# Decay products of a recurrent attention kernel from logarithms and a triangular product in place of scans

## The chip, the cores and the metric

One core of one Trainium2 chip. The metric is device time in microseconds of one launch; the median of three runs is quoted. The profile shows the core's engines: TensorE (PE, its weight loads apart as PEld), VectorE (DVE), ScalarE (ACT), GpSimd (POOL) and the DMA issuing queue of SyncE (SP). Each engine works through its own instructions strictly in their order and waits on semaphores for the others.

## The reference

First comes a recurrent attention over 768 steps for 4 batches of 8 heads with 40 by 40 states, then a mixture of experts, top 2 of 8, on its output:

```python
for t in range(S):                       # per batch and head
    y[:, :, t] = einsum('bhd,bhde->bhe', rt, state)
    Sa = einsum('bhde,bhe->bhd', state, at)
    state = state * wt[:, :, None, :] - einsum('bhd,bhe->bhde', Sa, bt) + einsum('bhd,bhe->bhde', vt, kt)
# x = y as rows [3072, 320]
noisy = x @ w_gate + log1p(exp(x @ w_noise)) * noise     # the router
top2, softmax over the two
out[rows of e] += weight * (relu(x @ w1[e]) @ w2[e])      # F = 1024
```

The decays w lie between 0.85 and 0.95. Inside a chunk of 64 steps the kernel needs the running products of w over time and their reciprocals.

## The kernel before

The 768 steps are cut into 12 chunks of 64; a **unit** is one chunk of half of the batches (16 batch-heads), so that there are 24 units, u = 0 to 23. Most work of a unit runs as products of 64 by 64 tiles of fp32, four tiles of the array at once. One pass of the loop in `run` is **stage n**; it works on unit n and prepares unit n+8 (`LP=8`). The order in which the calls are written in `run` is the order of every engine's instructions (the schedule is manual); loads are tied to ScalarE instructions (`after`, `s.ea`).

The path of a unit: `TA`, `TB` finish the inverse of a triangular matrix, `U` uses it, `UT` transposes the result, `P` multiplies with r, VectorE masks that (`pm`, L743), and `Y` of the same unit, at the start of the next stage, gives the output rows and the new state S. `RL` turns the output into rows and adds the router's logits. `AK`, `KBT`, `W1`, `W2`, `ST` feed these. TensorE and ScalarE alternate along this path: each product is evicted from PSUM by ScalarE before the next.

The decays: `scans` (L578 to L582) on VectorE makes the reverse running product B, the reciprocal of its ends, and the forward running product wq. `aprod` and `kprod` multiply a, k and b by these, and `LS` makes the matrix that is to be inverted; `LSe` evicts it by three ScalarE instructions out of PSUM. For four units at a time (a group) VectorE solves 32 by 32 triangles by 30 elimination steps of two operations each (`solve`, L619 and L620), spread over the four stages by the table `PLAN`, between a transposition into X (`xtr`) and two out of it (`tout`). The first group is solved in 16 by 16 halves (`solve16`) and completed by small products (`S16`) for each of its units.

Around the loop: `ramp` prepares units 0 to 4 and solves the first group; stage 0 then carries `S16` for units 1 to 3 and prepares units 5 to 8. The router (`gate_`, `route`) runs for 8, 4, 4, 4 and 4 units as a generator that is advanced by `m.rstep()` at three places of a stage. `warm` issues fp16 products on a zero tile, whose results nobody reads, on TensorE. Ten writes of zeros to the output (`zero`, 320 KB each) are issued in `ramp`, six later. After unit 23 the experts follow (from about 420 us), which the change doesn't touch.

## Time and profile before

| | |
|---|---|
| median of three runs | 832.08 us (830.48 to 838.36) |
| the profiled execution | 834.11 us, span 832.4 us |
| busy share of the span: PE, PEld, DVE, ACT, POOL | 87%, 63%, 67%, 44%, 37% |
| mean granted TensorE clock | 0.973 of 2.4 GHz |
| chain that ended last | PE 60%, DVE 22%, ACT 7%, issue 5%, DMA 2%, POOL 2% |
| the mask `pm` starts: units 1, 3, 9, 15, 23 | 86.35, 114.28, 200.24, 299.64, 417.19 us |

The start of the mask of unit n marks the end of stage n's TensorE path and is used as milestone throughout. A window of the profile gives busy time of each engine between two such marks; a timeline gives single instructions with their start, length and, in brackets, the idle time before them and what ended it. PE's records are two per fp32 product, and they overlap: the distance from start to start tells what a product costs.

### The profile page before, as it was taken

What the parts mean: (1) busy time and instruction counts of PE and PEld (TensorE: products, weight loads), DVE (VectorE), ACT (ScalarE), POOL (GpSimd) and SP (SyncE); (2) the same over time, 40 slices, a digit from 0 to 9 for tenths busy, and PEclk for the clock granted to TensorE, in tenths of its full rate; (3) what the DMA queues carried; (4) which work ended last, traced back from release to release, by engine and by line L of the source; (5) the groups of instructions that cost most, each with busy time, mean ns of one, the idle gap of its engine ahead of it and who ended that gap; (6) DMA issues with size and microseconds to landing.
All of it is one profiled execution on the core that took longest, in us unless ns stands there. A gap on an engine that the chain in (4) does not pass through costs nothing.

```text
span 832.4 us, 30024 instructions
## 1 busy us (share of the span) xinstructions
...
## 2 busy tenths in 40 slices
...
GB/s 214 242 182 59 153 135 151 155 143 119 108 114 117 114 94 90 66 127 122 68 96 65 163 70 154 144 141 93 142 29 149 75 124 120 36 18 24 29 17 40
DMA packets 67703, 89.54 MB, mean 108 GB/s; under 512 B 15640, under 2 KB 49388, under 8 KB 67564
## 3 DMA queue, kind: packets, MB, share of 16 engines
...
q0 software_dynamic: 12160, 17.15, 12.3%
q8 instruction: 105, 1.72, 0.9%
q14 instruction: 34, 0.28, 0.1%
HBM read 65.82 MB, written 21.69 MB: 105 GB/s over the span
## 4 chain that ended last, share of the span: by engine, by line
PE 60%; DVE 22%; ACT 7%; issue 5%; DMA 2%; POOL 2%; another core or an unknown queue 1%; SPq 0%; DVEq 0%; ACTq 0%; POOLq 0%
PE po L366 20%; PE ph L351 19%; DVE Tt L619 4%; DVE X__71 L620 3%; PE pp L740 3%; DVE pm L743 2%; PE kt L687 2%; PE pt L331 2%; PE py L760 2%; ACT la L523 2%; PE tb L673 2%; ACT tt L523 1%; DVE B L578 1%; PE ta L663 1%; DVE dr L623 1%
## 5 line engine op out<-in xcount | busy, mean ns | idle before, releaser
L374 POOL DMA_INDIRECT out_dram<-y,le x45 | 74.8, 1662 | 193.6 <-ACT y L368 189.4
L351 PE MATMUL ph<-rw__68,rk 128*128 128x384 f16 (+1 forms) x512 | 97.0, 339 | 3.6 <-DVE hl L353 1.7
L351 PE MATMUL ph<-dr,la 128*128 128x448 f16 (+1 forms) x384 | 86.7, 342 | 1.7 <-DVE rk L353 1.7
L366 PEld LDWEIGHTS <-rk 128*128 128x128 f16 x576 | 56.6, 100 | 38.5 <-issue 8.6
L179 POOL DMA_INDIRECT ls<-ent,po x48 | 48.6, 1013 | 77.8 <-ACT pm L523 43.2
L351 PEld LDWEIGHTS <-rk 128*128 128x128 f16 x512 | 49.4, 98 | 40.3 <-issue 4.1
L353 DVE SCALAR_TENSOR_TENSOR hl<-ph,hh 128x448 f16<-128x448 f32 x64 | 39.4, 623 | 48.1 <-ACT hh L352 46.1
L593 POOL TENSOR_TENSOR rk<-rk,B 104x512 f32<-104x512 f32 x32 | 37.9, 1184 | 85.2 <-DVE X__71 L620 36.0
L368 ACT ACTIVATE y<-po,le 128x320 f32<-128x320 f32 (+1 forms) x53 | 26.6, 504 | 94.1 <-PE po L366 75.2
L352 ACT ACTIVATE hh<-ph 128x448 f16<-128x448 f32 x64 | 34.2, 542 | 67.5 <-PE ph L351 64.0
L239 DVE TENSOR_REDUCE yc<-y 128x1 f32<-128x320 f32 (+1 forms) x53 | 23.9, 457 | 57.6 <-ACT y L368 52.0
L619 DVE TENSOR_TENSOR Tt<-X__71 128x30 f32<-128x30 f32 (+9 forms) x150 | 57.8, 385 | 4.1
L352 ACT ACTIVATE rk<-ph 128x384 f16<-128x384 f32 x64 | 30.8, 489 | 63.5 <-PE ph L351 48.0
L366 PEld LDWEIGHTS <-hh 128*128 128x128 f16 (+1 forms) x640 | 46.6, 103 | 18.7 <-issue 2.2
L353 DVE SCALAR_TENSOR_TENSOR rk<-ph,rk 128x384 f16<-128x384 f32 x64 | 34.3, 553 | 33.9 <-ACT rk L352 24.6
L351 PEld LDWEIGHTS <-la 128*128 128x128 f16 x384 | 37.6, 99 | 28.4 <-issue 3.0
L620 DVE TENSOR_TENSOR X__71<-X__71,Tt 128x30 f32<-128x30 f32 (+9 forms) x150 | 50.0, 333 | 5.5
L366 PE MATMUL po<-ra,rk 128*128 128x320 f16 x288 | 46.0, 306 | 3.0 <-ACT rk L352 2.5
L760 PE MATMUL py<-pm,kt 128*64 128x104 f32 (+1 forms) x768 | 42.0, 259 | 1.8 <-issue 0.9
L743 DVE TENSOR_TENSOR pm<-pp,mk 128x512 f32<-128x512 f32 x48 | 30.9, 685 | 16.0 <-PE pp L740 12.9
L600 PE MATMUL ls<-rk,ra 64*64 64x64 f32 x768 | 20.7, 251 | 23.9 <-DVE rk L593 8.7
L760 PEld LDWEIGHTS py<-pm,kt 128*64 128x64 f32 x768 | 36.2, 140 | 6.6 <-issue 3.1
...
## 6 DMA issues: line engine op xcount, KB each, us to landing
...
```

The costliest lines, as they stand in the source:

```text
L179: st=nc.gpsimd.indirect_dma_start(out=s.ls,out_offset=OFFS(ap=po[:,j,k:k+1],axis=0),in_=s.ent[:,j,k],in_offset=None)
L351: for i,(a,b) in enumerate(mm): s.hmm=nc.tensor.matmul(ph[:,:n],a,b,start=i==0,stop=i==7)
L352: s.hrelu=nc.scalar.activation(hh[:,f],ph[:,:n],AF.Relu)
L353: s.hhl=nc.vector.scalar_tensor_tensor(hl[:,f],ph[:,:n],0.0,hh[:,f],op0=ALU.max,op1=ALU.subtract)
L366: for j in range(c): nc.tensor.matmul(po[p*j:p*j+p,:d],h[:,f,r],w[:,f,d*j:d*j+d],start=k==0,stop=k==23)
L368: s.hy=nc.scalar.activation(y[:,:d],po[:,:d],AF.Copy,scale=w_[:,ii:ii+1])
L374: st=s.nc.gpsimd.indirect_dma_start(out=o[0],out_offset=OFFS(ap=o[1],axis=0),in_=o[2],in_offset=None,compute_op=ALU.add)
L593: s.after((eng or s.nc.gpsimd).tensor_tensor(z,z,b1,op=ALU.mult),e)
L619: eng.tensor_tensor(t,X[:,j:j+1,j+1:].to_broadcast([128,j,m]),X[:,0:j,j:j+1].to_broadcast([128,j,m]),op=ALU.mult)
L620: s.hs=eng.tensor_tensor(X[:,0:j,j+1:],X[:,0:j,j+1:],t,op=ALU.add)
L743: nc.vector.tensor_tensor(m[:,y,:,0:64],pp[:,y].rearrange("p (j t)->p j t",t=64),s.mk.to_broadcast([128,8,64]),op=ALU.mult)
L760: nc.tensor.matmul(pp[64*y:64*y+64,b,104*hh:104*hh+n],kt[:,j,y],m[:,y,j,0:n],start=first and hh==0,stop=True,skip_group_check=True)
```

## The change

It replaces the scans. The logarithm of w is taken on ScalarE (`ln`), a product with a 128 by 128 triangle of ones on TensorE sums it along time for all 8 heads of a unit (`sm`, four fp32 products of 128 by 128), and two exponentials on ScalarE give wq and B (`ex`). VectorE keeps the largest logarithm of each unit (`lc`) for the check at the end. w is loaded in another layout (160 KB a unit in place of 260).

Other edits: the second half of `LSe` is copied from the result in SBUF and moved later (`LSd`); the state is no longer added by an identity product but by VectorE, and scaled by GpSimd; `RL` uses four products of 128 rows in place of sixteen 64 by 64 tiles; the mask is one instruction; the router's arithmetic before the top 2 goes to GpSimd, save for the last four units; `PLAN` spreads the elimination steps otherwise, with a place C behind `Y`; the fill products in `UT` go where `sm` comes. `ramp` is rewritten, and stage 0 is a function of its own (`first`), written out by engine needs: `S16` of units 2 and 3 moves into stages 1 and 2, the first group's X is masked before its transposition, and six of the ten writes of zeros and the zeros of xd move into the loop.

```diff
+    def zx(s):
+        nc=s.nc; z=s.z; n=24-NA; return nc.sync.dma_start(s.xd[0][128*NA:3072].rearrange("(p a) (h d)->p (a h) d",p=128,h=2),z.rearrange("p (o d)->p o d",o=1).to_broadcast([128,2*n,DM//2]))
...
+        nc=s.nc; E=nc.vector if n0+T>=NT else nc.gpsimd
-        zc=r("zc"); nc.vector.tensor_scalar(zc,lg[:,:,8:16],41.0,None,op0=ALU.min)
+        zc=r("zc"); E.tensor_scalar(zc,lg[:,:,8:16],41.0,None,op0=ALU.min)
...
-PLAN={0:dict(A=range(1,8)),1:dict(B=range(8,11),A=range(11,15)),2:dict(B=range(15,19),A=range(19,25)),3:dict(B=range(25,31))}
+PLAN={0:dict(A=range(1,5)),1:dict(C=range(5,7),B=range(7,12),A=range(12,14)),2:dict(C=range(14,15),B=range(15,20),A=range(20,22)),3:dict(C=range(22,24),B=range(24,31))}
+PLAN1={1:dict(B=range(1,8),A=range(8,12)),2:dict(C=range(12,14),B=range(14,20),A=range(20,22)),3:dict(C=range(22,24),B=range(24,31))}
...
+        s.L=[t([128,4,2,64],F32,name="L"),s.uc]; s.TR=t([128,136],F32,name="TR")
+        G.memset(s.TR,0.0)
+        for b in range(2):
+            z=s.TR[64*b:64*b+64,64*b:64*b+64]; G.memset(z,1.0)
+            G.affine_select(out=z,in_=z,pattern=[[-1,64]],base=0,channel_multiplier=1,compare_op=ALU.is_ge,fill=0.0)
...
+    def ln(s,u):
+        s.act(s.L[u%2 if u<7 else 0][...,0:40],s.fl(s.wq[u%NW])[:,0:320].rearrange("p (h y e)->p h y e",h=4,y=2),AF.Ln)
+    def lc(s,u):
+        s.nc.vector.tensor_reduce(s.lm[:,u:u+1],s.L[u%2 if u<7 else 0][...,0:40].rearrange("p h y e->p (h y) e"),axis=AX.XY,op=ALU.max,apply_absolute_value=True)
+    def sm(s,u):
+        pp=s.Sp=s.p1t("sm"); L=s.L[u%2 if u<7 else 0]
+        for hh in range(4): s.nc.tensor.matmul(pp[:,128*hh:128*hh+128],L[:,hh].rearrange("p y e->p (y e)"),s.TR[:,0:128],start=True,stop=True)
+    def ex(s,u):
+        z=s.Sp.rearrange("p (j t)->p j t",t=64); B=s.B[u%2][:,0:520].rearrange("p (j c)->p j c",c=65)
+        s.act(s.wq[u%NW][:,:,0:64],z,AF.Exp,scale=-1.0)
+        s.act(B[:,:,0:64],z,AF.Exp)
+        s.nc.gpsimd.tensor_copy(s.gam[0:RF,u],B[0:RF,:,0])
     def scans(s,u):
...
+        s.ln(u); s.sm(u); s.ex(u)
...
     def LSe(s,u,pp):
         g,us=divmod(u,4); l=s.lab[g%2][:,8*us:8*us+8].rearrange("p (y h) t->p y h t",y=2); z=pp[:,:,0:256].rearrange("p y (h t)->p y h t",t=64)
         s.act(l,z,AF.Copy,scale=-1.0)
+    def LSd(s,u):
+        g,us=divmod(u,4); l=s.lab[g%2][:,8*us:8*us+8]
         for b in range(2):
-            r=slice(64*b,64*b+32); s.act(l[r,:,:,32:64],z[r,:,:,0:32],AF.Copy,scale=-1.0)
+            r=slice(64*b,64*b+32); s.act(l[r,:,32:64],l[r,:,0:32],AF.Copy)
...
     def UT(s,u):
-        nc=s.nc; pp=s.p1t("ut"); s.warm(pp,FU)
+        nc=s.nc
+        if u and u+LP<NU: s.sm(u+LP)
+        pp=s.p1t("ut")
+        if not u or u+LP>=NU: s.warm(pp,FU)
...
-        for y in range(2):
-            nc.vector.tensor_tensor(m[:,y,:,0:64],pp[:,y].rearrange("p (j t)->p j t",t=64),s.mk.to_broadcast([128,8,64]),op=ALU.mult)
+        nc.vector.tensor_tensor(m.rearrange("p y j x->p (y j) x")[...,0:64],pp.rearrange("p y (j t)->p (y j) t",t=64),s.mk.to_broadcast([128,16,64]),op=ALU.mult)
...
-            if not last:
-                for b in range(2):
-                    nc.tensor.matmul(pp[:,b,0:416].rearrange("p (h x)->p h x",x=104)[...,64:104],s.m.idm,S.rearrange("p (h b) d->p b h d",b=2)[:,b,:,0:40],start=False,stop=False,skip_group_check=True)
...
-            nc.vector.tensor_tensor(S.rearrange("p (h b) d->p b h d",b=2)[...,0:40],pv[...,64:104],gb,op=ALU.mult)
+            Sv=S.rearrange("p (h b) d->p b h d",b=2)[...,0:40]
+            if first: nc.vector.tensor_tensor(Sv,pv[...,64:104],gb,op=ALU.mult)
+            else:
+                nc.vector.tensor_tensor(Sv,pv[...,64:104],Sv,op=ALU.add)
+                nc.gpsimd.tensor_tensor(Sv,Sv,gb,op=ALU.mult)
...
     def RL(s,u):
         nc=s.nc; m=s.m; pp=s.p2("rl"); x=s.xt
...
+        for hh in range(4): nc.tensor.matmul(pp[:,0,128*hh:128*hh+96],x[:,2*hh:2*hh+2].rearrange("p b t->p (b t)"),s.iw[:,hh],start=True,stop=True)
+        v=pp[:,0].rearrange("p (h x)->p h x",x=128)
         xt=s.wk.tile([128,DM],F32,name="xr",bufs=2)
...
+        s.act(xt.rearrange("p (h e)->p h e",h=4),v[...,0:80],AF.Copy)
+        s.hl=nc.vector.tensor_reduce(m.logit(u),v[...,80:96].rearrange("p h l->p l h"),axis=AX.X,op=ALU.add)
...
+        s.lw(0); loads(0,1,2,3); LS={}
+        s.ln(0); s.sm(0); s.ex(0); s.ln(1); s.sm(1); gn(4); s.consts1(0)
         for u in range(4):
...
+            if u<3: s.ex(u+1)
+            s.aprod(u,V); s.kprod(u,1,None,V); s.kprod(u,0,None,V); s.lc(u)
+            if u==3: s.lc(4); V.tensor_reduce(s.m16,s.i32[:,16:32],axis=AX.X,op=ALU.add)
+            if u>1: s.lmask(u-2)
...
+            if u<3: s.ln(u+2); s.sm(u+2)
+            LS[u]=s.LS(u)
+            if u: LS[u-1](); s.LSd(u-1)
+        LS[3](); s.LSd(3); s.lmask(2); s.AK(0); s.lmask(3); s.ex(4); s.ln(5); s.sm(5); s.ex(5); s.xtr(0)
+        s.consts1(3); s.xmask16()
...
+        m.consts2(s.z)
+        s.KBT(0)(); s.consts16(); s.ln(6)
+        s.W1(0)
+        for z in s.vt+s.r+s.rb: s.null(z)
...
+        s.vc(0); m.marks()
...
+        m.consts3(); m.consts4()
         for i in range(ZR): m.zero(i,ZP)
...
+        s.solve16(); s.hA=s.hs; s.tout16(); s.first()
+    def vprods(s,u):
+        V=s.nc.vector; s.aprod(u,V); s.kprod(u,1,None,V); s.kprod(u,0,None,V)
+    def first(s):
+        nc,m=s.nc,s.m; V=nc.vector; H=s.lh
+        s.vprods(4); s.vprods(5); s.lc(5); s.lc(6)
+        s.S16a(0); s.S16b(0); s.sm(6); a4=s.LS(4); s.W2(0); s.ex(6); s.TA(0); a4(); s.ln(7); a5=s.LS(5); s.TB(0); s.vprods(6)
+        s.sm(7); a5(); s.U(0); s.LSd(4); k=s.KBT(1); s.UT(0); s.ex(7); s.lc(7); s.vprods(7)
+        a6=s.LS(6); s.LSd(5); k(); s.ln(LP); s.lc(LP)
+        s.P(0); s.S16a(1); a6(); s.LSd(6); s.AK(1); s.Y(0); a7=s.LS(7); s.S16b(1); s.sm(LP); a7(); s.LSd(7); s.ex(LP)
+        s.ld(H,1,'gv',s.vt)
+        s.xtr(1); s.xmask(); s.aprod(LP,V); s.kprod(LP,1,None,V)
+        s.W1(1); s.vc(1); s.hA=None
...
-            if ok(n-1): s.Y(n-1)
+            if n>1: s.Y(n-1); sv('C')
+            if n and not q and n<=20: m.rstep()
...
+            if n and ok(n+LP): s.ln(n+LP); s.lc(n+LP)
             if ls: ls()
+            if ls and not q: s.LSd(n+LP-1)
...
-            if n==0: s.S16(1); s.prep(5); s.scans(6)
...
-            if n and ok(n+LP): s.scans(n+LP); s.aprod(n+LP)
...
-            if ok(n+LP): s.kprod(n+LP,1,s.hl if ok(n-1) else None)
+            if n and ok(n+LP): s.ex(n+LP); s.kprod(n+LP,1)
             if ok(n+1): s.W1(n+1)
             if ok(n): s.P(n)
-            if n==0: s.S16(3)
+            if ok(n+LP): s.aprod(n+LP)
+            if n<3: s.S16(n+1)
...
+            if n==ZN+ZP-ZR: s.after(m.zx(),s.ea)
...
-ZN,ZP,ZR=2,16,10
+ZN,ZP,ZR=2,16,4
```

Three places show the order. VectorE, in a stage that is the first of a group, from the new state S to the mask `pm`; `akm` is the mask of `AK`, `lg` the logits. Before:

```order
L765 TENSOR_TENSOR S_108<-py,gam 128x2x4x40
L766 TENSOR_TENSOR xT<-py,rw__68 128x2x4x64
L578 SCALAR_TENSOR_TENSOR B_111<-rw__68,d_118 104x520
L580 RECIPROCAL d1f<-B_111 104x8
L582 SCALAR_TENSOR_TENSOR rw__68<-rw__68,d1f 104x520
L684 TENSOR_TENSOR akm<-ak,mk 128x512
L609 STREAM_TRANSPOSE X__71<-la 128x1024
L777 TENSOR_REDUCE lg<-rl 128x16
L743 TENSOR_TENSOR pm_101<-pp,mk 128x8x64 x2
```

and now:

```order
L790 TENSOR_TENSOR S_108<-py,S_108 128x2x4x40
L792 TENSOR_TENSOR xT<-py,rw__68 128x2x4x64
L586 TENSOR_REDUCE lm<-L 128x1
L707 TENSOR_TENSOR akm<-ak,mk 128x512
L625 STREAM_TRANSPOSE X__71<-la 128x1024
L799 TENSOR_REDUCE lg<-rl 128x16
L768 TENSOR_TENSOR pm_101<-pp,mk 128x16x64
```

The two scans (printed as SCALAR_TENSOR_TENSOR) and the reciprocal are gone; `lm`, the largest logarithm, stands in their place.

TensorE, between `KBT` (`kt`) and `W1` (`pw`) of a stage with LP units ahead. Before:

```order
L687 MATMUL kt<-idm,rk 128x128 x8
L560 LDWEIGHTS d_118
L560 MATMUL ut<-d_118 128x512
L560 LDWEIGHTS d_118
L560 MATMUL ut<-d_118 128x512
L719 MATMUL ut<-idm,uc 128x128 x4
L773 MATMUL rl<-iw,xT 64x64 x16
L695 MATMUL pw<-v_99,akm 64x40 x16
```

and now:

```order
L710 MATMUL kt<-idm,rk 128x128 x8
L589 MATMUL sm<-TR,L 128x128 x4
L745 MATMUL ut<-idm,uc 128x128 x4
L795 MATMUL rl<-iw,xT 128x96 x4
L718 MATMUL pw<-v_99,akm 64x40 x16
```

The fill products of `ut` have given way to the four sums `sm`, and `rl` is four products.

ScalarE, at the end of the first group's preparation, from the eviction of `KBT` (behind the writes `dr<-idm`, in both) up to the first eviction of `S16` (`w1s<-sa`). Before:

```order
L523 ACTIVATE kt_103<-kt 128x16x40
L523 ACTIVATE la<-ls 128x512
L523 ACTIVATE la<-ls 32x8x32 x2
L523 ACTIVATE pm_101<-v_98 64x8x40 x2
L631 ACTIVATE w1s<-w1s 128x32x16 x2
L631 ACTIVATE w1s<-w1s 128x16x16
L632 ACTIVATE w1s<-la,w1s 128x32x16
L523 ACTIVATE w1s<-sa 128x8x16
```

and now:

```order
L524 ACTIVATE kt_103<-kt 128x16x40
L650 ACTIVATE w1s<-w1s 128x32x16 x2
L650 ACTIVATE w1s<-w1s 128x16x16
L651 ACTIVATE w1s<-la,w1s 128x32x16
L524 ACTIVATE L<-rw__68 128x8x40
L544 ACTIVATE vt<-z 128x512
L544 ACTIVATE r_92<-z 128x512
L544 ACTIVATE r_93<-z 128x512
L544 ACTIVATE rb_94<-z 128x512
L544 ACTIVATE rb_95<-z 128x512
L524 ACTIVATE pm_101<-v_98 64x8x40 x2
L524 ACTIVATE w1s<-sa 128x8x16
```

The five clears of vt, r and rb, which stood early in `ramp`, and a logarithm now stand ahead of that eviction.

## Rows read from the trace of the kernel before

**Rows 1.** Windows of four stages: length, PE, PEld, DVE, ACT, POOL busy, clock, DMA

```profile
86.35:114.28 27.93, 24.51 (x786) 19.93 (x785) 26.55 (x58) 14.57 (x34) 6.85 (x8) 1.00 0.48 142
114.28:200.24 85.96, 76.75 (x2463) 62.88 (x2462) 76.25 (x151) 44.10 (x105) 29.15 (x32) 1.00 0.49 145
200.24:299.64 99.40, 83.42 (x2474) 68.97 (x2473) 88.83 (x240) 44.18 (x107) 41.89 (x55) 0.93 0.39 111
299.64:417.19 117.55, 105.95 (x3035) 82.85 (x3034) 78.99 (x212) 59.45 (x139) 34.20 (x55) 1.00 0.34 96
```

**Rows 2.** Timeline of VectorE in stage 12: start us, us, line, operation

```profile
256.36 1.23 DVE L578 TENSOR_TENSOR_SCAN B<-rw__68,d 104x520 f32<-104x520 f32 x1
...
257.86 1.24 DVE L582 TENSOR_TENSOR_SCAN rw__68<-rw__68,d1f 104x520 f32<-104x520 f32 x1
...
259.60 0.98 DVE L619 TENSOR_TENSOR Tt<-X__71 128x184 f32<-128x184 f32 x1
260.61 0.35 DVE L620 TENSOR_TENSOR X__71<-X__71,Tt 128x184 f32<-128x184 f32 x1
...
262.50 0.18 DVE L201 SCALAR_TENSOR_TENSOR d<-w,u 128x32 f32<-128x32 f32 x1
```

**Rows 3.** Timeline of GpSimd, same stretch

```profile
259.18 1.19 POOL L587 TENSOR_TENSOR ra<-ra,rw__68 104x512 f32<-104x512 f32 x1 [1.34 <-DVE rw__68 L582]
```

**Rows 4.** Waits of TensorE, 86 to 200 us: us in total, times, longest

```profile
PE kt L687 <- ACT la L523: 4.7, 8, 0.6
```

**Rows 5.** Waits of TensorE, 200 to 300 us

```profile
PE tb L673 <- DVE wq L220: 2.9, 1, 2.9
```

**Rows 6.** Timeline of TensorE, stages 4 and 5

```profile
130.62 0.81 PE L754 MATMUL py<-S,idm 128*128 128x160 f32 x4
131.36 1.65 PE L760 MATMUL py<-pm,kt 128*64 128x104 f32 x32
...
139.37 0.59 PE L560 MATMUL ut<-d 128*128 128x512 f16 x2
139.80 0.60 PE L719 MATMUL ut<-idm,uc 128*128 128x128 f32 x4
140.33 0.69 PE L773 MATMUL rl<-iw,xT 64*64 64x64 f32 x32
140.85 0.63 PE L695 MATMUL pw<-v,akm 64*64 64x40 f32 x32
```

**Rows 7.** Timeline of VectorE at the start

```profile
27.41 1.93 DVE L609 STREAM_TRANSPOSE X__71<-la 128x1024 f32<-128x1024 f32 x1 [1.75 <-ACT la L523]
...
32.28 0.19 DVE L638 TENSOR_TENSOR Tt<-X__71 128x28 f32<-128x28 f32 x1 [1.08 <-POOL X__71 L612]
```

**Rows 8.** Timeline of ScalarE at the start

```profile
28.37 4.25 ACT L556 ACTIVATE dr<-idm 32x1024 f32<-32x1024 f32 x4
...
43.75 0.28 ACT L523 ACTIVATE w1s<-sa 128x128 f32<-128x128 f32 x1 [6.08 <-PE sa L650]
...
53.38 0.28 ACT L523 ACTIVATE w1s<-sa 128x128 f32<-128x128 f32 x1 [2.64 <-remote]
```

**Rows 9.** Timeline of TensorE, end of stage 0

```profile
69.94 0.94 PE L650 MATMUL sa<-dr,w1s 32*32 32x16 f32 x55
...
73.89 3.04 PE L760 MATMUL py<-pm,kt 128*64 128x104 f32 x32
```

**Rows 10.** Groups of instructions, whole run: busy us, mean ns, idle before

```profile
L523 ACT ACTIVATE tt<-tb 128x512 f32<-128x512 f32 x24 | 14.3, 597 | 27.1 <-PE tb L673 27.1
...
L523 ACT ACTIVATE pm<-v 64x320 f32<-64x320 f32 x48 | 22.4, 467 | 0.6
...
L593 POOL TENSOR_TENSOR rk<-rk,B 104x512 f32<-104x512 f32 x32 | 37.9, 1184 | 85.2 <-DVE X__71 L620 36.0 <-DVE lg L777 35.8 <-DVE l L213 9.8
```

**Rows 11.** Windows around one fall of the clock

```profile
285.00:290.00 5.00, 2.70 (x109) 2.06 (x102) 4.73 (x16) 1.19 (x3) 1.17 (x1) 0.87 0.33 112
290.00:295.00 5.00, 4.85 (x93) 4.17 (x87) 4.83 (x9) 3.14 (x7) 1.68 (x3) 0.50 0.20 59
```

More of the change, by code (lines that the diff above doesn't have):

```diff
@@ L545, in consts1 @@
             for z in s.kt: G.memset(z,0.0)
+            G.memset(s.mk32,1.0)
+            for q in range(4): G.affine_select(out=s.mk32[32*q:32*q+32,0],in_=s.mk32[32*q:32*q+32,0],pattern=[[-1,32]],base=0,channel_multiplier=1,compare_op=ALU.is_gt,fill=0.0)
+            G.memset(s.d1,0.0)
         if i==1:
+            for q in range(4): G.tensor_copy(s.i32[32*q:32*q+32],s.m.idm[32*q:32*q+32,32*q:32*q+32])
             for z in s.w: G.memset(z,0.0)
@@ L551, in consts1 @@
         if i==3:
-            for q in range(4): nc.scalar.activation(s.i32[32*q:32*q+32],s.m.idm[32*q:32*q+32,32*q:32*q+32],AF.Copy)
             for b in range(2):
@@ L562, in lw @@
     def lw(s,u):
-        s.last=s.nc.sync.dma_start(s.fl(s.wq[u%NW]),s.A['gw'][u].rearrange("y p x->(y p) x")); return s.last
+        s.last=s.nc.sync.dma_start(s.fl(s.wq[u%NW])[:,0:320],s.A['gw'][u]); return s.last
     def lh(s,n,sl,u,y=None):
-        z=s.fl(sl[u%len(sl)])
+        z=s.fl(sl[u%len(sl)][:,0:8])
         for b in ((y,) if y is not None else range(2)):
@@ L644, in tout16, with S16a @@
         V.transpose(s.dg[:,:,16:32].rearrange("p k s->p s k"),X[:,16:32])
-        for b in range(2): s.nc.gpsimd.memset(s.dg[64*b+32:64*b+64,:,0:32],0.0)
+        for b in range(2): V.memset(s.dg[64*b+32:64*b+64,:,16:32],0.0)
     def S16(s,u):
+        s.S16a(u); s.S16b(u)
+    def S16a(s,u):
         nc=s.nc; z=s.Zw[u%2]; Q=[slice(32*q,32*q+32) for q in range(4)]; g=lambda p: p.rearrange("p (k c)->p k c",c=16); us=slice(8*u,8*u+8)
@@ L651, in S16, with S16b @@
         s.act(z[:,:,16:32],g(pp[:,0:128]),AF.Copy)
+    def S16b(s,u):
+        nc=s.nc; z=s.Zw[u%2]; Q=[slice(32*q,32*q+32) for q in range(4)]; g=lambda p: p.rearrange("p (k c)->p k c",c=16); us=slice(8*u,8*u+8)
         pq=s.p1t("sb")
@@ L804, in ramp, with gn, loads @@
-        s.KBT(0)(); s.scans(4)
-        s.xtr(0); s.xmask16(); s.aprod(4,V)
-        for x in range(2): s.kprod(4,x,None,V)
-        V.tensor_reduce(s.m16,s.i32[:,16:32],axis=AX.X,op=ALU.add)
-        s.LS(4)(); s.W1(0); s.vc(0); s.consts16()
-        m.consts2(s.z); m.marks()
-        for i in range(ZR): m.zero(i,ZP)
-        m.consts3()
-        s.solve16(); s.hA=s.hs; s.tout16(); s.S16(0)
+        def gn(*u):
+            for i in u: G.memset(s.a[i],0.0); G.memset(s.kb[i%NKB],0.0)
+        def loads(*us):
+            e,s.ea=s.ea,None
+            for u in us: load(u); s.lw(u+1)
+            s.ea=e
@@ new lines, in ramp @@
+        LS[3](); s.LSd(3); s.lmask(2); s.AK(0); s.lmask(3); s.ex(4); s.ln(5); s.sm(5); s.ex(5); s.xtr(0)
+        s.consts1(3); s.xmask16()
+        s.ea=None; s.lv(0); loads(5,6)
+        m.consts2(s.z)
+        s.KBT(0)(); s.consts16(); s.ln(6)
+        s.W1(0)
+        for z in s.vt+s.r+s.rb: s.null(z)
+        s.ea=None; H('gv',s.vt,0); H('gr',s.r,0); H('grb',s.rb,0); s.lv(1); load(7); s.lw(8); load(8)
+        for y in range(2): nc.sync.dma_start(s.iw[64*y:64*y+40].rearrange("p h x->p (h x)"),s.A['iw'][y])
@@ L817, in run @@
         s.ramp()
-        for n in range(NU):
+        for n in range(1,NU):
             g,q=divmod(n,4)
@@ L821, in sv @@
             def sv(p):
-                if solving and p in PLAN[q]: s.solve(V,PLAN[q][p])
+                pl=PLAN1 if n<4 else PLAN
+                if solving and p in pl.get(q,()): s.solve(V,pl[q][p])
             def sc(k):
@@ L863, in run @@
             cut()
-            if n==0: s.prods(6)
             kb=s.KBT(n+1) if ok(n+1) else None
             if ok(n): s.UT(n)
+            if n==1: ls=s.LS(LP); ls()
             if kb: kb()
+            if ls and q: s.LSd(n+LP-1)
             cut()
             s.ld(H,n+1,'gr',s.r)
-            if n==0: s.S16(2); s.prep(7); s.scans(LP); s.AK(1); s.aprod(LP)
             if solving and q==0: s.xtr(g+1); s.xmask()
-            if n==NU-1: s.turn(0)
+            if n==NU-1: s.turn(0); s.act(s.gt[:,8*NU:9*NU],s.lm,AF.Exp)
             sv('B')
```

112 lines of the change are left out of this document (43 added, 69 removed).

## The prediction, made before the changed kernel was run

> **What bounds the kernel now.** I read the windows between milestones first [rows 1]. The columns to compare are PE, DVE and the length. In stages 4 to 9 (the second line) the two engines are level: 76.75 and 76.25 of 85.96 us, so a stage takes 14.3 us and holds 12.8 us of TensorE and 12.7 us of VectorE work. In stages 10 to 15 (third line) a stage takes 16.6 us; VectorE works 88.83 of 99.40, 14.8 a stage, because the router has come on top, and TensorE's granted clock falls to 0.93. In stages 16 to 23 no unit is prepared any more; TensorE works 105.95 of 117.55 and VectorE 67%.
>
> The timeline of VectorE says what its time is spent on: the two scans of a stage are 1.23 and 1.24 us [rows 2]. The waits of TensorE come next. Up to 200 us the largest is 0.6 us in each stage, KBT waiting for ScalarE's eviction of LS [rows 4]. Beyond, it is VectorE: TB once waits 2.9 us, until VectorE has left a router step and released a PSUM buffer [rows 5]. Last the clock: from 285 us TensorE is busy for 2.70 of 5 us, and in the 5 us after that it is granted 0.50, which is 1.2 GHz [rows 11]. So VectorE sets stages 10 to 15, directly and through the clock; TensorE with its alternation with ScalarE sets the others. The experts behind unit 23 are not touched, and I let them follow rigidly.
>
> **VectorE, stages 1 to 15.** Each loses two scans, 2.47 us (the reciprocal, shorter than any row here, is left out). It gains the largest logarithm, a reduction of 128x320 that the trace doesn't show: between an operation of 128x184, 0.35 us, and a transposition of 128x1024, 1.93 us [rows 2, 7]; I take 0.5, near the first. Ten router operations like the 0.18 us one [rows 2] leave it once in four units, 0.5 a stage. The new addition replaces a multiplication of the same size, and one mask replaces two halves: nothing. So 12.7 becomes 10.7 in stages 4 to 9, and 14.8 becomes 12.3 in stages 10 to 15, both below TensorE's work.
>
> **TensorE, stages 1 to 15.** The identity product of the state goes: from 130.62 to the next start at 131.36, 0.74 us. The fill products of UT go: 139.37 to 139.80, 0.43. In comes sm, eight records of 128 rows by 128 columns. From below they cost what UT's four transpositions of that size do, 139.80 to 140.33, or 0.13 each; from above the identity product's 0.74 for four records of 160 columns, 0.185 each. I take 0.13, since the columns are the same: 1.06 us. RL had 32 records in 0.52 us (140.33 to 140.85) [rows 6]; its eight records of 96 columns cost 0.73 by Y's pace (32 records of 104 columns in 1.65, two side by side in the array) and 1.48 by the identity product's; I take 0.8, near the first, as Y's columns are nearest. Together +0.17: 13.0 us a stage. The idle time beside it was 85.96 less 76.75, 1.5 a stage. Of that the wait for LS's eviction shrinks: one instruction of 0.6 instead of three releases the buffer, though a logarithm now stands in front; I take 0.3 off, and another 0.3 for small waits on VectorE. That leaves 0.9 and a stage of 13.9.
>
> Stages 4 to 9 then take 6 x 13.9 = 83.4, **2.6 less**. Stages 10 to 15 have the router's small products as well; with VectorE at 12.3 it is still not idle for long, so I take 14.2: 85.2, **14.2 less**. That includes the clock, since its falls follow VectorE's late stages. Stages 16 to 23 lose the identity product and gain 0.28 in RL, 13.24 to 12.8 of work, with 1.5 of idle time as before: 14.3 instead of 14.7, **3.2 less**.
>
> **ScalarE and GpSimd in the loop.** ScalarE gains a logarithm (0.47, by the eviction of 64x320) and two exponentials (0.60 each, by TB's eviction of 128x512) [rows 10], 1.7 us on 44.10/6 = 7.4 of 13.9 us. They cost nothing as long as they stand behind what P needs (uc, utm, kt) and ahead of what only the next Y needs; that is where they are written. If they were on the path they would cost 1.2 us a stage. GpSimd gains the scaling of S (320 of 512 elements of a 1.18 us product [rows 10]: 0.7 us) and the router's operations, on 7.0 us a stage. It is covered by the next use of S one stage later; LS, a stage later too, waits for the last of three products, with about 1.5 us to spare by my count. The six writes of zeros are 320 KB each, one a stage, where the DMA engines are busy for 0.48 [rows 1]; w's loads shrink: nothing.
>
> **The start.** Before, X is transposed at 27.41 us, and the first elimination step begins at 32.28, after GpSimd's mask [rows 7]. Five units' scans, 12.3 us, leave VectorE ahead of the transposition; ScalarE gets about 3 us a unit (logarithm, exponentials, evictions of LS) in their place. If that replaces them one for one nothing is won (27.4); if it is hidden, 12 us. Since ScalarE works on one unit while VectorE works on another, I take 22. Then follow 2 us of transposition and no mask: first step at 24.3, first S16 product at 34.7. But ScalarE is not free then: 4.25 us of writes [rows 8], KBT's eviction, four copies, a logarithm, five clears and two evictions, some 7 us at 0.47 to 0.60 each, from about 25.7: 37.4 instead of 43.75, **6.4 less**. From there to unit 1's mask it was 42.6 us. Two of four S16 leave: the last ran from 69.94 to 73.89 [rows 9], partly at the lower clock; I take 3.4 each, and they return in stages 1 and 2, so that this moves the milestone by 6.8 and the end by nothing. A wait of 2.64 us of S16's eviction on a transfer [rows 8] should go, since lists and zeros are issued later and fewer; new ScalarE work for units 6 to 8 (5 us) takes back about 1.9. **0.7 less**.
>
> **Sum.** 7.1 + 2.6 + 14.2 + 3.2 = 27.1 us. Against the profiled execution's 834.1 that is 807.0; it lay 2.0 above the median of 832.1, so I forecast **805 us**. Milestones: unit 1's mask at 72.4, unit 3's at 107, unit 9's at 191, unit 15's at 276, unit 23's at 390.
>
> **Rivals.** (A) *More at the start, and denser stages.* If ScalarE's preparation doesn't hold S16 back (X transposed nearer to 18) and a stage takes 13.5, TensorE's work and half of the idle time: another 9 us, 796. For it: TensorE's remaining waits are each small. Against: TensorE and ScalarE still alternate.
>
> (B) *GpSimd becomes the late engine.* An elimination step of 184 elements took 0.98 us while a GpSimd product ran and its neighbour of equal size 0.35 [rows 2, 3]: 0.63 lost. If each of the four GpSimd products of a stage (4.3 us) stopped VectorE for its whole length, VectorE would need 12.3 + 4.3 less the 0.6 already in it, 16 us, in stages 10 to 15, and their gain falls to 3.4: 816. The Trainium skill (SBUF — State Buffer, Who interferes with whom) says just that: a VectorE instruction with two SBUF inputs and a GpSimd instruction that reads SBUF exclude each other for a whole instruction. By that rule the one row agrees; whether all four hit such operations no row shows, and masks and S read PSUM.
>
> (C) *The change doesn't do what it says:* VectorE's time was on nobody's path, or comes back as TensorE work. With sm and RL at 0.185 a record a stage holds 14.1 and takes 15.4: stages 4 to 9 lose 6.4, stages 10 to 15 win 7.0, stages 16 to 23 lose 1.7, and the start keeps 4.7: 828. Against it: the records of 128 columns.
>
> (D) *Slower: the clock.* The fills leave UT in stages 1 to 15. A Y at 0.50 took 3.04 us for 32 records, 1.65 at full clock [rows 6, 9], so a stage of 13 us of TensorE work grows by 11 at the lower level. 2.5 such stages eat the gain, and from 3.3 on it is slower by more than 1%; four give 849. For it: the fall in rows 11 follows a TensorE that was half idle. Against: the clock is 1.00 in stages 2 to 9, and sm stands where the fills stood.
>
> **Chances and range.** The forecast 0.50 (798 to 812), A 0.20, B 0.14, C 0.07, D 0.05, others 0.04. The range from 792 to 820 leaves out C, D and the edges. A measurement of this kernel tells about 1% from no change, here 8.3 us: faster 0.86 (the forecast, A, B), same 0.09 (C and a weaker B), slower 0.05 (D).
>
> **What would show it.** The milestones above; between units 9 and 15 a VectorE busy share near 87% and a clock near 1.00; sm's records 0.13 apart, RL's eight in 0.8; KBT's wait below 0.3. Were TB still waiting for VectorE there, the VectorE step is wrong; were LS waiting for a GpSimd product, B is at work; X's transposition later than 25 us, or S16's first eviction at 43, makes the start wrong.

## The result, and the profile after

The changed kernel takes 826.93 us in the median of 10 runs (817.96 to 829.86) against 834.82 us of the kernel before (830.48 to 838.36); the ratio is 0.9886, with an interval from 0.9857 to 0.9915. The forecast was 805 us with a range from 792 to 820. The direction was right; of 27 us forecast, 8 came. In two later comparisons the unchanged file had ratios of 0.9892 [0.9869, 0.9915] and 0.9896 [0.9859, 0.9933].

The first profiled execution lasted 817.96 us, the shortest of all; three later ones lasted 820.08, 829.49 and 823.78 us. The columns below use the mean of these four, 822.8 us, 15.8 above the 807.0 that the forecast's sum gave for a profiled execution. The other 4 us up to the median are differences between executions of the same code.

| | before | forecast | mean of four |
|---|---|---|---|
| up to the mask of unit 1 | 86.4 | 72.4 | 77.6 |
| stages 2 and 3 | 27.9 | 34.6 | 36.5 |
| stages 4 to 9 | 86.0 | 83.4 | 82.3 |
| stages 10 to 15 | 99.4 | 85.2 | 93.2 |
| stages 16 to 23 | 117.6 | 114.3 | 116.8 |
| behind unit 23, to the span's end | 415.2 | as before | 414.4 |

Windows of the first profiled execution, cut at the masks of units 1, 3, 9, 15 and 23, answer to [rows 1] (same columns):

```profile
77.33:112.87 35.54, 31.96 (x1065) 27.80 (x1057) 25.52 (x58) 19.00 (x49) 8.28 (x9) 0.90 0.36 105
112.87:195.56 82.69, 76.54 (x2329) 66.23 (x2328) 66.22 (x125) 52.93 (x124) 37.30 (x48) 1.00 0.50 147
195.56:287.00 91.44, 79.42 (x2343) 68.39 (x2342) 80.40 (x211) 54.28 (x129) 46.77 (x70) 0.98 0.52 150
287.00:403.20 116.20, 104.78 (x2814) 83.68 (x2813) 75.36 (x185) 59.30 (x140) 49.33 (x85) 0.97 0.36 96
```

Stages 4 to 9 are what was forecast: 82.69 us, with 76.54 us of TensorE. In stages 10 to 15 VectorE was to be busy for 12.3 us a stage and is for 80.40/6 = 13.4; stages 2 and 3 have a mean clock of 0.90.

TensorE in stage 10 answers to [rows 6]; the distance from start to start is the price:

```profile
204.35 1.09 PE L710 MATMUL kt<-idm,rk 128*128 128x128 f32 x8 [0.28 <-ACT la L524]
205.28 1.06 PE L589 MATMUL sm<-TR,L 128*128 128x128 f32 x8
206.17 0.60 PE L745 MATMUL ut<-idm,uc 128*128 128x128 f32 x4
206.61 1.03 PE L795 MATMUL rl<-iw,xT 128*128 128x96 f32 x8
207.57 0.68 PE L718 MATMUL pw<-v,akm 64*64 64x40 f32 x32
```

`sm` costs 0.89 us (1.06 taken) and `RL` 0.96 (0.8 taken): 1.85 together, 1.86 in the forecast. VectorE in the same stage answers to [rows 2], GpSimd to [rows 3]:

```profile
195.56 1.23 DVE L768 TENSOR_TENSOR pm<-pp,mk 128x1024 f32<-128x1024 f32 x1
196.70 1.27 DVE L635 TENSOR_TENSOR Tt<-X__71 128x228 f32<-128x228 f32 x1
198.00 1.26 DVE L636 TENSOR_TENSOR X__71<-X__71,Tt 128x228 f32<-128x228 f32 x1
199.30 0.40 DVE L635 TENSOR_TENSOR Tt<-X__71 128x234 f32<-128x234 f32 x1
...
201.14 0.68 DVE L792 TENSOR_TENSOR xT<-py,rw__68 128x512 f32<-128x512 f32 x1
```

```profile
196.53 1.19 POOL L607 TENSOR_TENSOR rk<-rk,B 104x512 f32<-104x512 f32 x1
197.67 1.34 POOL L601 TENSOR_TENSOR ra<-ra,rw__68 104x512 f32<-104x512 f32 x1
```

Behind the mask `pm` two halves of an elimination step take 1.27 and 1.26 us, the next, a little larger, 0.40. The two long ones lie beside GpSimd's two products, which end at 197.72 and 199.01, and each ends 0.25 us behind one of them. The same operation takes 0.40 us at 209.04, with no product beside it. Behind them stands `xT`, which releases the PSUM buffer that TB waits for, and this wait has the largest total of TensorE's waits in stages 10 to 15 (columns as in [rows 4]):

```profile
PE tb L696 <- DVE xT L792: 4.7, 5, 1.3
```

The start, TensorE, VectorE and ScalarE (answers to [rows 7, 8]):

```profile
3.90 2.04 PE L589 MATMUL sm<-TR,L 128*128 128x128 f32 x8 [3.90 <-POOL lm L539]
8.11 2.08 PE L589 MATMUL sm<-TR,uc 128*128 128x128 f32 x8 [2.16 <-ACT uc L524]
...
43.33 2.08 PE L589 MATMUL sm<-TR,L 128*128 128x128 f32 x8
...
50.10 1.16 PE L589 MATMUL sm<-TR,L 128*128 128x128 f32 x8 [0.43 <-ACT L L524]
```

```profile
25.85 1.94 DVE L625 STREAM_TRANSPOSE X__71<-la 128x1024 f32<-128x1024 f32 x1
...
28.26 0.15 DVE L657 TENSOR_TENSOR Tt<-X__71 128x28 f32<-128x28 f32 x1
```

```profile
40.22 0.94 ACT L524 ACTIVATE pm<-v 64x320 f32<-64x320 f32 x2
41.18 0.28 ACT L524 ACTIVATE w1s<-sa 128x128 f32<-128x128 f32 x1
```

A sum `sm` lasts 2.04 to 2.08 us at the start. The first record of the granted clock stands at 23 us, so it says nothing on most of them. But the sum at 43.33, where the granted clock is 0.50, lasts 2.08 as well, and the one at 50.10, at 1.00, takes 1.16. So I read the sums at the start as running at the lower level. X is transposed at 25.85 us (22 forecast, 27.41 before), the first step follows at 28.26 (24.3), and S16's first eviction stands at 41.18 (37.4; before 43.75), right behind ScalarE's clears and copies, as the step on ScalarE said.

### The profile page after: what moved, and what is told of

It reads as the page before. It is cut to its first block, busy times and chain, and to the rows that moved or that the text cites. A ratio compares the mean times of both kernels' runs of the same rounds, so it can differ in the third digit from the quotient of the medians.

```text
span 816.0 us, 29101 instructions
## 1 busy us (share of the span) xinstructions
PE 728.5 (89%) x12619; PEld 537.9 (66%) x12619; DVE 516.5 (63%) x1083; ACT 391.0 (48%) x837; POOL 337.8 (41%) x463
## 4 chain that ended last, share of the span: by engine, by line
PE 67%; DVE 14%; ACT 10%; issue 5%; DMA 2%; another core or an unknown queue 0%; SPq 0%; POOL 0%; ACTq 0%; DVEq 0%; POOLq 0%
PE po L369 21%; PE ph L354 21%; PE py L782 3%; PE sm L589 2%; PE pt L334 2%; DVE Tt L635 2%; DVE X__71 L636 2%; PE kt L710 2%; DVE pm L768 2%; PE tb L696 2%; PE pp L766 2%; ACT la L524 2%; PE ta L686 1%; PE rl L795 1%; DVE dr L639 1%
## 5 line engine op out<-in xcount | busy, mean ns | idle before, releaser
L636 DVE TENSOR_TENSOR X__71<-X__71,Tt 128x30 f32<-128x30 f32 (+9 forms) x150 | 60.8, 405 | 5.5
L635 DVE TENSOR_TENSOR Tt<-X__71 128x30 f32<-128x30 f32 (+9 forms) x150 | 60.8, 406 | 3.7
L594 POOL COPY gam<-B 104x8 f32<-104x8 f32 x24 | 5.3, 220 | 105.7 <-ACT B L524 104.9
L369 PE MATMUL po<-w2h,rk 128*128 128x320 f16 x192 | 33.7, 302 | 3.7 <-issue 2.6
```

The costliest lines, as they stand in the source:

```text
L369: for j in range(c): nc.tensor.matmul(po[p*j:p*j+p,:d],h[:,f,r],w[:,f,d*j:d*j+d],start=k==0,stop=k==23)
L635: eng.tensor_tensor(t,X[:,j:j+1,j+1:].to_broadcast([128,j,m]),X[:,0:j,j:j+1].to_broadcast([128,j,m]),op=ALU.mult)
L636: s.hs=eng.tensor_tensor(X[:,0:j,j+1:],X[:,0:j,j+1:],t,op=ALU.add)
```

## The experiments

**The changed kernel again.** Three repeats show how much executions of the same code differ; the last of them stands beside other kernels on the same chip.

> The changed kernel as it is, to have a second profiled execution of it: the first lasted 818.0 us where its runs have a median of 826.9. Theory (the clock): the second execution is near 827 us, its mean granted clock near 0.957 instead of 0.966, and the 9 us lie in added stretches at 0.50 of the clock, in the loop or the experts; the milestones outside of such stretches agree to 0.5 us. Rival (a transfer or an engine that starts late): the clock is the same as in the first and one milestone interval is longer by some us with a wait that the first does not have.

> The changed kernel as it is, a third profiled execution: the first two lasted 818 and 820 us, where the median is 827. Theory (clock): if it is near 827 us, the additional time lies in stretches at the lower level behind unit 16 (the steps put behind xT gave a profile with 121.4 us for stages 16 to 23 and 416.2 for the rest, against 116.2 and 412.8). Rival: it lies in one wait on a transfer.

> The changed kernel as it is, beside the three that follow, on their chip: stages 4 to 9 at 82 to 83 us, stages 10 to 15 at 91 to 94, with 12 to 15 us lost by VectorE to GpSimd's products in the latter.

They lasted 820.08, 829.49 and 823.78 us. The 829.49 one differs from the first in several places by 1 to 5 us each: stage 1 by 1.8, stage 3 by 1.7, stage 14 by 2.4, the part behind unit 23 by 4.7; the granted clock fell more often (twice instead of once between units 9 and 17), and stage 14 has a wait that the first execution does not have. The second and fourth execution have it as well. VectorE, GpSimd and TensorE of the second in stage 14:

```profile
254.38 3.01 DVE L636 TENSOR_TENSOR X__71<-X__71,Tt 128x228 f32<-128x228 f32 x1
257.43 0.40 DVE L635 TENSOR_TENSOR Tt<-X__71 128x234 f32<-128x234 f32 x1
...
268.52 0.17 DVE L226 CAST xf<-ix 128x8 f32<-128x8 uint32 x1
268.73 2.53 DVE L228 TENSOR_TENSOR oh<-io,xf 128x64 f32<-128x64 f32 x1
```

```profile
254.81 1.19 POOL L607 TENSOR_TENSOR rk<-rk,B 104x512 f32<-104x512 f32 x1
255.94 1.19 POOL L601 TENSOR_TENSOR ra<-ra,rw__68 104x512 f32<-104x512 f32 x1
...
268.86 1.17 POOL L607 TENSOR_TENSOR rk<-rk,B 104x512 f32<-104x512 f32 x1
269.99 1.17 POOL L601 TENSOR_TENSOR ra<-ra,rw__68 104x512 f32<-104x512 f32 x1
```

```profile
271.61 0.21 PE L155 MATMUL pr<-cnt,tri 128*128 128x32 f16 x1 [3.07 <-DVE cnt L152]
```

One step on X takes 3.01 us, beside two products that follow each other; the router's `oh`, 0.22 us elsewhere, takes 2.53 beside the next pair, and TensorE stands for 3.07 us at the router's `pr`. So neither of the two theories was right alone: both the falls of the clock and this wait differ between executions.

**The steps behind xT.** Place A of the table was emptied into place C:

```diff
-PLAN=...1:dict(C=range(5,7),B=range(7,12),A=range(12,14)),2:dict(C=range(14,15),B=range(15,20),A=range(20,22)),3:dict(C=range(22,24),...
+PLAN=...1:dict(C=range(5,7),B=range(7,12)),2:dict(C=range(12,15),B=range(15,20)),3:dict(C=range(20,24),...
```

> The elimination steps that stand directly behind the mask pm in the second and third stage of a group are put behind xT (place A to place C). Theory (VectorE against GpSimd at one place): behind the mask two steps of 0.40 us take 1.2 us each while GpSimd multiplies for the next unit, and hold back xT, for which TB waits 4.7 us in stages 10 to 15; without them there TB does not wait, stages 10 to 15 shorten by 4 to 6 us, and the whole by 4 to 8 against the changed kernel. Rival (VectorE has too much to do, wherever it stands): xT is in time but the mask or lm is late by the same amount, and the time changes by less than 2 us.

826.77 us, 0.9878 [0.9851, 0.9906]: no change in the whole. At the place itself the theory holds: TB waits 0.8 in place of 4.7 us, and stages 10 and 11 take 14.39 and 14.22 instead of 15.03 and 14.88. But `pr` waits 3.1 us in stage 14, as it does in the three repeats without this edit (here the pair of products meets the router's `ent`, which takes 2.31 us), and the clock fell twice. Stages 10 to 15 take 92.60, against 93.2 in the mean of four.

**The fills in UT.**

```diff
-        if not u or u+LP>=NU: s.warm(pp,FU)
+        s.warm(pp,FU)
```

> The two fp16 fill products come back in UT in all stages, beside sm. Theory (the fills held the clock): of the falls in stages 1 to 15 of the changed kernel at most one is left, and the time falls by 2 to 6 us although 15 x 0.43 = 6.5 us of TensorE work come in. Rival (the fills do nothing for the clock that sm doesn't do): as many falls, and the time rises by 4 to 7 us.

828.48 us, 0.9912 [0.9889, 0.9936]. Between units 3 and 17 the clock did not fall once (one to three falls in the repeats), stages 10 to 15 took 91.03; but stages 4 to 9, which have no falls anyway, took 85.99 instead of 82.3. Both theories were half right: the falls are gone here, and the fills cost as much as that saves. That the fills hold the clock rests on this one execution; one without them (the identity product, below) had no fall between units 3 and 17 either.

**The logarithms first at the start.**

```diff
...
-            if u<3: s.ex(u+1)
-            s.aprod(u,V); s.kprod(u,1,None,V); s.kprod(u,0,None,V); s.lc(u)
+            s.lc(u)
+            if u<3: s.ln(u+2); s.ex(u+1); s.sm(u+2)
+            s.aprod(u,V); s.kprod(u,1,None,V); s.kprod(u,0,None,V)
...
```

> At the start the logarithm of unit u+2 is taken ahead of the exponentials of unit u+1, with its own sum right behind, and w is loaded ahead of a and k, so that the sums of two units follow each other on TensorE. Theory (the chain ln, sm, ex of 3.7 us a unit, in which sm takes 2.08, holds the transposition into X at 25.9 us): VectorE's 3.1 us a unit are left, X is transposed at 23 to 24, the first eviction of S16 lies at 39 instead of 41.2, and the whole is 1.5 to 3 us shorter. Rival (loads or VectorE set the pace of the start): X is transposed within 0.7 us of 25.9 and the time does not change.

822.81 us, 0.9836 [0.9801, 0.987]; the changed kernel took 827.13 beside it. TensorE, VectorE and ScalarE of that kernel:

```profile
3.90 2.05 PE L589 MATMUL sm<-TR,L 128*128 128x128 f32 x8 [3.90 <-POOL lm L539]
5.97 2.07 PE L589 MATMUL sm<-TR,uc 128*128 128x128 f32 x8
...
10.47 1.16 PE L589 MATMUL sm<-TR,uc 128*128 128x128 f32 x8
```

```profile
21.12 1.96 DVE L625 STREAM_TRANSPOSE X__71<-la 128x1024 f32<-128x1024 f32 x1
```

```profile
36.45 0.28 ACT L524 ACTIVATE w1s<-sa 128x128 f32<-128x128 f32 x1
```

The chain theory holds: with the sums back to back the fourth takes 1.16 us, X is transposed at 21.12 (the forecast's 22) and S16's first eviction stands at 36.45 (37.4). But unit 3's mask came at 113.3 in this execution: stages 1 and 2 took 21.92 and 19.91 us at mean clocks of 0.77 and 0.83, where the first execution of the changed kernel had 0.91. Where in the program the 4 us of the medians lie, this one profile does not show.

**Fills around S16**, alone and with both edits above:

```diff
-        pp=s.p1t("sa")
+        pp=s.p1t("sa"); s.warm(pp,3)
...
```

> On the changed kernel: three fp16 fill products ahead of each of the two products of S16, and sixteen on TensorE while it waits for the first group's elimination. Theory (stages 0 to 3 are long because the granted clock falls behind TensorE's idle 7 us and behind each S16): S16 of unit 0 runs at the higher level, at most two falls are left up to unit 3's mask, which lies at 106 to 109 instead of 112.3 to 112.9, and the whole is 3 to 6 us shorter. Rival (the fills only add TensorE work, some 0.21 to 0.43 each): as many falls, unit 3's mask at 114 to 117.

> The fills of the run before this together with the logarithms taken first at the start and the steps put behind xT. Theory (the start's gain of 4.7 us at the first S16 was given back by falls of the clock in stages 0 to 2, and the steps cost where they stood): unit 3's mask at 101 to 105, stages 10 to 12 at 14.2 to 14.4 each, the whole 815 to 820 us in the median. Rival (something else, such as a load, holds unit 3 at 112 to 113 whatever is ahead of it): unit 3's mask stays there, and the median at 822 to 827.

827.92 us, 0.9906 [0.9873, 0.9939], and 824.82 us, 0.9877 [0.985, 0.9903]. The theory fails in both, and unit 3's mask comes even later than the rivals had it: 118.6 and 114.0. Between units 1 and 3 one fall is left in place of the changed kernel's two, yet these stages take 37.1 and 36.5 us, no less than its 36.5. Windows of 2 us in stage 1 of the second kernel show something else:

```profile
58.00:60.00 2.00, 1.41 (x93) 1.13 (x93) 0.21 (x1) 0.00 (x0) 0.00 (x0) 1.00 1.04 280
60.00:62.00 2.00, 0.00 (x0) 0.00 (x0) 0.00 (x0) 0.00 (x0) 0.00 (x0) 0.93 0.12 30
62.00:64.00 2.00, 1.57 (x10) 1.53 (x10) 0.00 (x0) 1.21 (x4) 0.00 (x0) 0.50 0.04 8
```

The DMA engines are full up to 60 us. Then no engine works for 2 us: TensorE stands for 2.9 us in the middle of S16's small products, with nothing in the profile that it waits for ("issue"), and the clock falls to 0.50.

**The scans back on VectorE** as dummies (the shape of the work, its results unused):

```diff
+                z=s.wk.tile([128,240],F32,name="Tt",bufs=1); V.memset(z,0.0)
+                for _ in range(4): V.tensor_tensor_scan(z[0:RF],z[0:RF],...
...
```

> On the changed kernel VectorE gets, in each stage that prepares a unit, the work of the two scans back as dummies on a scratch tile behind xT: one clear and four scans of 104x240, about 2.5 us. Theory (the scans were on the path only where VectorE is the later engine): stages 4 to 9 grow by 0 to 0.4 us each, stages 10 to 15 by 1.5 to 2.5 each, the whole by 10 to 16 us, to 837 to 843. Rival (VectorE's time was on nobody's path): under 4 us in all.

846.85 us, 1.0135 [1.0101, 1.017], where the changed kernel has 0.989: some 20 us more. The profiled execution is the longest of its four (852.64):

```profile
116.10:208.58 92.48, 78.72 (x2330) 66.73 (x2328) 84.95 (x156) 54.31 (x127) 41.01 (x51) 0.98 0.47 139
208.58:316.83 108.25, 86.11 (x2342) 73.06 (x2342) 100.15 (x240) 52.80 (x125) 46.61 (x68) 0.92 0.42 121
```

Stages 4 to 9 grow by 1.7 us each, more than expected, stages 10 to 15 by 2.5. With this load VectorE's time is on the path in both, with 85 of 92 us busy in the former. The dummies are somewhat longer than what they stand for: 3.3 and 3.1 us a stage, where scans and reciprocal took 2.9 in the kernel before.

**GpSimd's products to VectorE**, right behind the mask, with the steps behind xT:

```diff
...
-            if ok(n+LP): s.aprod(n+LP)
+            if ok(n+LP): s.vprods(n+LP)
```

> With the steps put behind xT, the three products of unit n+8 that GpSimd makes (1.18 us each) go to VectorE, right behind the mask, where it waits for Y; there they take 0.6 each. Theory (a VectorE instruction with two inputs in SBUF stands still while a GpSimd product runs; 12 to 14.6 us were lost so in stages 10 to 15 of the changed kernel): this loss falls below 3 us in stages 10 to 15, VectorE's busy time falls in spite of 1.9 us more a stage, no TensorE product waits 3 us for the router, and stages 10 to 15 take 86 to 89 us instead of 91.4 to 93.7; the whole is 4 to 8 us below the changed kernel. Rival (VectorE's added 11 us weigh as much as the loss): stages 10 to 15 take 91 to 96.

806.35 us against 812.67 of the kernel before, which takes 20 us less on this chip than elsewhere: 0.9906 [0.9875, 0.9938]. The changed kernel itself was not run on this chip; elsewhere it has 0.989, so no gain of the whole shows. Stages 10 to 15:

```profile
205.01:293.67 88.66, 78.24 (x2343) 67.90 (x2342) 79.40 (x228) 54.27 (x128) 26.50 (x51) 0.98 0.53 152
```

88.66 us. I call loss what VectorE's instructions that overlap a GpSimd product last beyond the shortest of the same line and shape. It is 0.8 us in these stages, where the four executions of the changed kernel lose 11.0 to 12.8, the kernel before 5.7, and the one with the steps behind xT 8.7. The theory holds in these stages. But the stages behind the two transpositions out of X (4, 8, 12, 16) grew to 16.4 to 17.6, since the products stand ahead of them and TA waits (2.8 us once).

**The products behind the mask, on GpSimd.**

```diff
...
-            if n and ok(n+LP): s.ex(n+LP); s.kprod(n+LP,1)
+            if n and ok(n+LP): s.ex(n+LP)
...
-            if ok(n+LP): s.aprod(n+LP)
+            if ok(n+LP): s.kprod(n+LP,1,s.hm); s.aprod(n+LP)
```

> With the steps put behind xT, the second and third of GpSimd's products are issued only behind the mask of the stage. Theory (they run ahead of a late mask and stop the router's VectorE work there, 2.5 us in place of 0.25, for which TensorE waits 3.1 us in stage 14 or 15): this wait is gone, and stages 14 and 15 together take 31 to 33 us in place of 33 to 35; the rest stays. Rival (the products come too late for LS in the next stage): TensorE waits at LS for GpSimd, 0.5 us or more in each stage, and stages 4 to 9 take 84 or more.

800.79 us, 0.9848 [0.9814, 0.9882]. The 3.1 us wait is gone, stages 14 and 15 take 32.1 together; LS did not wait. The theory holds.

**Two other parts of the change undone alone.** The identity product of the state back:

```diff
...
-                nc.vector.tensor_tensor(Sv,pv[...,64:104],Sv,op=ALU.add)
-                nc.gpsimd.tensor_tensor(Sv,Sv,gb,op=ALU.mult)
+            nc.vector.tensor_tensor(Sv,pv[...,64:104],gb,op=ALU.mult)
```

> On the changed kernel the state is again added by an identity product on TensorE and scaled by VectorE in one operation; GpSimd's scaling goes. Theory (TensorE sets a stage and this edit took 0.74 us of it): 22 stages grow by 0.3 to 0.7 us, the whole by 7 to 14. Rival (the scaling on GpSimd costs more than it saves, because it blocks VectorE and comes late): the whole is 0 to 5 us shorter.

805.60 us, 0.9911 [0.9882, 0.994], within the changed kernel's interval; stages 4 to 9 grew to 85.4 (0.5 a stage, as the theory said), but the theory's 7 to 14 us in the whole do not show. And the router's arithmetic on VectorE (`E=nc.vector`):

> On the changed kernel the router's arithmetic ahead of the top 2 is VectorE's again for all units. Theory (VectorE is the later engine in stages 10 to 15): these take 2 to 5 us more, for ten operations of 0.18 us in each group of four and their waits. Rival (GpSimd's router work blocks VectorE as much as it spares it): within 2 us.

800.61 us, 0.9828 [0.9786, 0.9869]; stages 10 to 15 took 92.7, no more than without that edit (93.2): the rival. No gain of moving the arithmetic to GpSimd shows.

**All together.** GpSimd keeps the products in the fourth stage of a group only; then with the logarithms first and the router's arithmetic on VectorE; then with the four writes of zeros in the loop as well:

```diff
...
+            if ok(n+LP): s.aprod(n+LP) if q==3 else s.vprods(n+LP)
...
-ZN,ZP,ZR=2,16,4
+ZN,ZP,ZR=2,16,0
```

> As with the three products on VectorE behind the mask, but in the fourth stage of a group, where two transpositions stand there that TensorE waits for, GpSimd keeps them. Theory (loss to GpSimd's products is what the forecast of 14.2 us a stage left out): stages 4, 8, 12 and 16 are back at 14.3 to 15, stages 10 to 15 take 86 to 88 us, stages 4 to 9 take 80 to 83, the whole is 0.98 or less of the kernel before, against 0.989 of the changed kernel. Rival (the clock takes it back): more falls than in the changed kernel, and 0.985 or more.

> The same with the logarithms taken first at the start and the router's arithmetic back on VectorE. Theory (these were worth 0.5% and 0.6% by themselves): 0.965 to 0.975 of the kernel before. Rival (they share one cause with the products, GpSimd's blocking, and the start's gain is lost by unit 3): as without them, within 0.3%.

> The same, and the four writes of zeros that were left in the start (1.3 MB) go into the loop too. Theory (behind the start the DMA engines are full, at 1.0 busy from 54 to 60 us in the run with all of the start's edits, TensorE then has no instructions for up to 2.9 us, and its clock falls): stage 1 shrinks from 21 to 23 us to 18 or 19, unit 3's mask comes 2 to 4 us earlier. Rival (loads, not zeros, fill the DMA engines): no change.

Beside the changed kernel's 824.03 us (0.9896) on this chip they took 819.31, 818.08 and 818.33 us: 0.985 [0.9815, 0.9885], 0.9839 [0.9806, 0.9872] and 0.9829 [0.9799, 0.986]. Stages 10 to 15 of the changed kernel and of the first of the three:

```profile
197.07:291.25 94.18, 81.17 (x2348) 69.98 (x2346) 79.31 (x211) 53.67 (x128) 45.72 (x67) 0.96 0.49 142
```

```profile
193.07:281.13 88.06, 78.51 (x2348) 67.19 (x2346) 79.74 (x225) 53.84 (x128) 30.02 (x52) 1.00 0.52 152
```

6.1 us less with as much VectorE work, at 30 instead of 46 us of GpSimd; the loss is 2.5 us, `pr` waits 0.7 us for the router in place of 3.1, and the clock does not fall. The first theory holds in these stages; the whole came out at 0.985, the rival's figure, though without its added falls. For the logarithms and the router the rival holds (0.1%). In the profiled execution of the second kernel unit 1's mask stands at 72.4 and unit 3's at 107.9, the forecast's 72.4 and 107; from unit 23 on it took 418.2 us, against 414.4 in the mean of four. Windows at the start of the second kernel (first line) and of the third:

```profile
56.00:58.00 2.00, 2.00 (x121) 1.80 (x120) 1.09 (x2) 0.00 (x0) 0.00 (x0) 1.00 1.21 211
```

```profile
56.00:58.00 2.00, 2.00 (x137) 1.77 (x131) 1.11 (x3) 0.00 (x0) 0.00 (x0) 1.00 0.03 8
...
64.00:66.00 2.00, 2.00 (x80) 1.96 (x78) 0.65 (x2) 1.07 (x2) 1.51 (x2) 0.50 0.52 148
```

The zeros did fill the DMA engines: without them the share at this place is 0.03 instead of 1.21, and TensorE does not lack instructions there. But the clock falls all the same (0.50 from 62.6 us, while TensorE waits 2.1 us at TB for ScalarE), and unit 3's mask stands at 111.3. So full DMA engines are not what the clock's fall needs; in the second kernel, with full ones, it did not fall here.

## Why the prediction was wrong

Two steps failed: the term of VectorE's 12.3 us a stage in stages 10 to 15, and the 22 us at which X was to be transposed. Falls of the clock came on top. The steps, with the distance from the forecast in the mean of four executions:

- **The start, 5.2 us too late at unit 1.** The step that failed is "Since ScalarE works on one unit while VectorE works on another, I take 22". As it is written, ln, sm and ex of one unit follow those of the unit before, 3.7 us a unit, and sm, 2.04 to 2.08 us each here, stood in no term of it. X was transposed at 25.85 in the first execution and at 25.0 in the mean, and S16's first eviction stood at 41.18 and 40.1 instead of 37.4: 2.7 of the 5.2 us. With the logarithms first both came where the forecast had them (shown). The other 2.4 us lie behind that eviction: from there to the mask it is 37.4 us instead of the forecast's 35.0. In this stretch the four executions spend 9.5 to 14.7 us at the lower level of the clock; the second of the three kernels put together spends 5.1 there and takes 35.2. So this part goes with the clock; no run changed the clock alone.
- **Stages 2 and 3, 1.9 us too late.** S16 was expected to come back at 3.4 us each. In all four executions the clock falls within 4 us behind it, and 6.8 to 10.2 us pass at the lower level. The run with the steps behind xT happened to have no fall here and took 35.0 us, 0.4 above the forecast; so the price of S16 was about right, and the falls were left out. Fills did not help (shown). What makes the clock fall here is open.
- **Stages 4 to 9, 1.1 us better:** TensorE's two new prices were right together to 0.01 us, by luck: one was 0.17 us too high, the other 0.16 too low. VectorE's loss rose here too, from 4.8 to 8.4 us, and cost nothing: with it at 0.9 us, in the first of the three kernels put together, these stages take 82.5.
- **Stages 10 to 15, 8.0 us too late,** the largest miss. The term that failed is VectorE's 12.3 us a stage. It counted the loss beside GpSimd's products as "already in it", as large as before; it rose from 5.7 us to between 11.0 and 12.8, by 1.1 a stage, and 12.3 became 13.4. TB's wait for xT is the sign that the prediction had named for this. In the kernel before, `kprod` waited at this place for the logits, and `aprod` stood well ahead of it, behind the scans; now the two follow each other at the mask and run beside the elimination steps of place A. That the products make the loss is shown (0.8 without them); that their new place raised it is read from the profiles, and with the steps elsewhere it is 8.7. This is rival B's mechanism at a place which its text did not name, and without its sign, a wait of LS; B had 0.14. The Trainium skill (SBUF — State Buffer, Who interferes with whom) has the rule that an instruction of VectorE with two inputs in SBUF contends with one of GpSimd that reads SBUF, and the traces agree: an instruction of 0.40 us lasted 3.01. VectorE's busy time alone does not set these stages, for it is as long (79.7 us) where they take 88.06. With the products taken off, their loss, the router's wait and the falls went together, worth 6.1 us on one chip (88.06 against 94.18) and 5.2 against the mean of four. The 2.9 us from there to the forecast stay open.
- **Stages 16 to 23, 2.5 us too late:** TensorE stood without instructions inside TA and Y for 2.5 us in stage 22 of the first execution (17.19 us, before 14.69), and the clock fell behind it (0.50 from 381.8 us). With the router's arithmetic on VectorE that stage took 15.00 and 15.04 us, beside 17.37 and 18.47 without on the same chip. On the chip where the kernel before takes 812.67 us it took 13.0 to 13.7 in four variants, with the arithmetic on either engine; why is open.
- **The clock without the fills (rival D)** does not decide: with the fills back the falls between units 3 and 17 go and the time does not.
- The median lies 4 us above the profiled executions' mean; before, the two agree within 1 us. The changed kernel varies more, by falls and waits that come and go in the same code.

That VectorE's time had a price was right: dummies of 3.1 to 3.3 us a stage cost some 20 us, where the forecast had 17 for what stages 4 to 15 would win. How much the scans' removal won by itself, apart from the new order of GpSimd's products and the clock, no run shows. The direction came out as reasoned. That unit 1's and unit 3's masks stood at the forecast's 72.4 and 107 in one later profile is no proof of the sum: it took other edits and few falls.
